# Attention with the top 32 keys and a highway layer: score tiles that are kept, and a dependency of last-row products on one of two top-eight passes taken off

## The chip, the cores and the metric

The kernel runs on one core of one Trainium2 chip. The metric is the time of one execution on the device in microseconds; the time of a kernel is the median of several executions. Times inside an execution come from one profiled execution of it.

## The reference

Queries, keys and values have 8 batches of 8 heads of 576 rows of 64 numbers. For each query row only the 32 largest scores take part in the softmax. The result of all heads, 4608 rows of 512, goes through a highway layer with two 512x512 weights.

```python
scores = scale * np.matmul(q, k.transpose(0, 1, 3, 2))
kth = np.partition(scores, -top_k, axis=-1)[..., -top_k:-top_k + 1]
mask = scores >= kth
scores = np.where(mask, scores, -1000000000.0)
scores = scores - np.max(scores, axis=-1, keepdims=True)
attn = np.exp(scores)
attn = attn / (np.sum(attn, axis=-1, keepdims=True) + 1e-09)
x = np.matmul(attn, v)          # then heads side by side: [4608, 512]
H = np.maximum(x @ w_h, 0.0)
T = 1.0 / (1.0 + np.exp(-(x @ w_t + b_t)))
out = T * H + (1.0 - T) * x
```

## The kernel before

**Units and pairs.** 576 query rows are four blocks of 128 rows and a last block of 64. A unit is what fills 128 partitions: a full block of one head, or the last 64 rows of two heads, one on partitions 0 to 63 and one on 64 to 127. Two units make a pair, and the text calls them the first and the second item of the pair. A batch has 16 pairs of full blocks and then 2 pairs of last rows, 18 in all; the kernel has 144 pairs, of which 16 are pairs of last rows.

**The score tile.** A pair's scores are written by TensorE into one PSUM tile `xs` of three banks of 512 numbers. The first item has columns 0 to 575: all of the first bank, and 64 columns of the middle one. The second item has the last 576 columns: 64 of the middle bank, and all of the third. There are two such tiles, taken in turn from the pool `xps`, so pair g has the tile that pair g - 2 had.

**One step.** The kernel is a pipeline with one step per pair, written out by hand; the program keeps the order in which it is written (`tc.manual_schedule`). In step i each engine does, in this order among others:

- TensorE (PE): the mask matmuls of pair i (`mask_add`, L419), which add a mark to all scores above a threshold; the products of probabilities and values of pair i - 3 (L509); matmuls without a use that keep its clock up (`spare`, L279); transposes of keys or queries for the next batch (L251); the score products of pair i + 2 (`scores`); one piece of the highway layer (L537); spares again.
- VectorE (DVE): twelve top-eight instructions over 96 columns each for pair i + 1 (`segs`, L358); a full top-eight over all 576 columns of each item of pair i (`below`, L432, two MAX8 in a row, first item first); the threshold of pair i + 1 (`refine`, L375 to L391); the selection of the 32nd score (L438, L451); the masked probabilities of pair i - 1 (L471).
- ScalarE (ACT): the exponentials of pair i (L424), the copy of the scores of pair i + 1 from PSUM (L353), the marks of pair i + 1 (`mask_count`, L406), the comparison for pair i - 1 (L454), copies of PE's other results (L523 for the value products, L252 for transposes, L624 and L648 for the highway layer).
- GpSimd (POOL): comparisons, the element-wise part of the highway layer, and the issue of some DMAs. SyncE issues most DMAs, the transposing ones for probabilities and for the layer's input `xT` among them.

**Around the change.** `below` of pair i needs the mask matmuls of pair i. It is the last reader of pair i's score tile: its first MAX8 reads the first and the middle bank, its second the middle and the third. Directly behind it in program order `start_scores(i + 2)` calls `scores`, which takes the tile anew for pair i + 2. A tile taken from a pool waits until all that used its predecessor is done; so the first product waits for both MAX8 of `below` and for PE's own mask matmuls.

For a pair of full blocks `scores` writes the two items in turn, 256 columns at a time (L311), and then the 64 end columns of both with one matmul (L322). For a pair of last rows it writes the first item, four matmuls of 256 columns into the first bank (L328; the profile counts each twice) and two of 64 columns into the middle bank (L339), and then the same for the second item into the third and the middle bank. The list `rest` and `declare_no_dep` in `segments` already let the twelve top-eight instructions of the first item start before the rest of the products is written; the tracker of dependencies otherwise goes by more than the columns that are used.

The lines of `finish` take the two score tiles again for the last highway blocks (`x1`, `x2`), and those of `begin` for the first transposes (`xa`). The code behind `tc.If` computes everything once more in a slower way where a check at the end asks for it, and is not run with these inputs.

Of the kernel before, what the change touches and what calls it, by code (L numbers as in the profile page):

```python
# [11 lines left out]
FP32 = mybir.dt.float32  # L12
# [14 lines left out]
def kernel(  # L27
# [10 lines left out]
    nc = tc.nc  # L38
    P = nc.NUM_PARTITIONS
# [13 lines left out]
    BANK = 512  # L53
# [13 lines left out]
    pairs = [(u, u + 1) for u in range(0, NU, 2)]  # L67
# [10 lines left out]
    xpool = ctx.enter_context(tc.tile_pool(name="x", bufs=3))  # L78
    fpool = ctx.enter_context(tc.tile_pool(name="f", bufs=2))
    hpool = ctx.enter_context(tc.tile_pool(name="h", bufs=3))  # L80
    xps = ctx.enter_context(tc.tile_pool(name="xps", bufs=2, space=bass.MemoryType.PSUM))
    ops = ctx.enter_context(tc.tile_pool(name="ops", bufs=1, space=bass.MemoryType.PSUM))
    fps = ctx.enter_context(tc.tile_pool(name="fps", bufs=1, space=bass.MemoryType.PSUM))


    ident_f = consts.tile([P, P], FP32)
# [12 lines left out]
    TOP, THR, KTH = 0, 1, NPK + 1  # L99
    wall = consts.tile([P, NU + 2, NPK + 2], FP32)  # L100
# [174 lines left out]
    def spare(n):  # L275
        if "t" not in po:
            po.update(t=pso_tile(), n=0)
        for _ in range(n):
            nc.tensor.matmul(  # L279
                po["t"][:, 4 * DE : BANK],  # L280
                ident_b[:],
                cst[:, 0 : BANK - 4 * DE],
                start=True,
                stop=True,
                skip_group_check=True,
            )

    def prep_alloc(kd):
        kT = kqpool.tile([P, NP, MAIN], FP32, name="kT")
        qT = kqpool.tile([P, NP, S], FP32, name="qT")  # L290
        return kT, qT, kd
# [2 lines left out]

    def scores(pair, prep):
        kT, qT, kd = prep
        ps = xps.tile([P, 3 * BANK], FP32, tag="x", name="xs")
        heads2 = [units[u][2] for u in pair]  # L300
        qt = units[pair[0]][1]
        qs = qt * P
        MB = 2 * BANK
        rest = []
        RA, RB = BANK, 2 * BANK - rem
        if qt < nfull:
            hp = heads2[0][0] // 2
            for n0 in range(0, MAIN, 256):
                for s, mo in ((0, 0), (1, MB)):
                    r = s * D  # L310
                    mm = nc.tensor.matmul(  # L311
                        ps[:, mo + n0 : mo + n0 + 256],
                        qT[r : r + D, hp, qs : qs + P],
                        kT[r : r + D, hp, n0 : n0 + 256],
                        start=(n0 == 0),
                        stop=True,
                        skip_group_check=True,
                    )
                    if s:
                        rest.append(mm)  # L320
            ends = ps[:, BANK:MB].rearrange("p (a n) -> p a n", n=rem)[:, 0 :: BANK // rem - 1, :]
            rest.append(nc.tensor.matmul(ends, qT[:, hp, qs : qs + P], kd[:, hp, :], start=True, stop=True))  # L322
        else:
            for (mo, ro), hh in zip(((0, RA), (MB, RB)), heads2):
                hp = hh[0] // 2
                for n0 in range(0, MAIN, 256):
                    for r in (0, D):
                        mm = nc.tensor.matmul(  # L328
                            ps[r : r + rem, mo + n0 : mo + n0 + 256],
                            qT[r : r + D, hp, qs : qs + rem],  # L330
                            kT[r : r + D, hp, n0 : n0 + 256],
                            start=(n0 == 0),
                            stop=True,
                            skip_group_check=True,
                        )
                        if mo:
                            rest.append(mm)
                for r in (0, D):
                    mm = nc.tensor.matmul(  # L339
                        ps[r : r + rem, ro : ro + rem],  # L340
                        qT[r : r + D, hp, qs : qs + rem],
                        kd[r : r + D, hp, r : r + rem],
                        start=(mo == 0),
                        stop=True,
                        skip_group_check=True,
                    )
                    rest.append(mm)
        both = bass.AP(tensor=ps.tensor, offset=ps[:].offset, ap=[ps[:].ap[0], [3 * BANK - S, 2], [1, S]])
        return ps[:, 0:S], ps[:, 3 * BANK - S : 3 * BANK], both, rest
# [49 lines left out]
    def biases(g):  # L399
        return nc.gpsimd.tensor_tensor(be[:, g], wall[:, 2 * g : 2 * g + 2, TOP : KTH + 1 : KTH - TOP], fac[:], ALU.mult)  # L400
# [22 lines left out]
    def expo(u, sc, e):  # L423
        nc.scalar.activation(e, sc, AF.Exp, bias=tb(u), scale=scale)  # L424
        return e
# [3 lines left out]
        return [t[:, s, :] for s in range(2)] + [t]  # L429

    def below(u, ps):
        nc.vector.max(wall[:, u, THR + 1 : KTH], ps)  # L432


    def hits(pair):
# [83 lines left out]
    def pso_tile():  # L519
        return ops.tile([P, BANK], FP32, tag="po", name="pso")  # L520
# [192 lines left out]
    preps = {0: prep_alloc(kds[0])}  # L713
# [4 lines left out]
    st = {}  # L718
# [4 lines left out]
    def ensure_prep(b, hp):  # L723
        for it in ((b, hp, 0), (b, hp, 1), (b, 0, 7), (b, 0, 8)):
            if it not in done:
                done.add(it)
                prep_piece(stages[b], preps[b], *it[1:])()
# [10 lines left out]
    def start_scores(g):  # L738
        b = units[pairs[g][0]][0]
        for u in pairs[g]:  # L740
            for h in units[u][2]:
                ensure_prep(b, h // 2)
        st[g] = dict(ps=scores(pairs[g], preps[b]), sc=[None, None], et=[None, None], e=[None, None])
        st[g]["seg"] = 0
        st[g]["cand"] = cands[g % len(cands)]

    def copy_both(g):
        st[g]["sc"] = copy_scores(st[g]["ps"][2])


    def segs(g, n):
        if g >= NG:
            return
        for c in range(st[g]["seg"], min(2 * NSEG, st[g]["seg"] + n)):
            s, k = divmod(c, NSEG)
            segments(st[g]["cand"][:, s], st[g]["ps"][s], k, k + 1, () if s else st[g]["ps"][3])
        st[g]["seg"] += n
# [27 lines left out]
    def masks_of(g):  # L785
        pr = pairs[g]
        views = (st[g]["ps"][0], st[g]["sc"][1])
        st[g]["m"] = [mask_count(u, views[s]) for s, u in enumerate(pr)]

    def step(i):  # L790
# [5 lines left out]
        b, k_in = divmod(i, SPB)  # L796
# [15 lines left out]
        if live:  # L812
            pr = pairs[i]
# [18 lines left out]
        segs(i + 1, 2 * NSEG)  # L832
        if live:
            below(pr[0], st[i]["ps"][0])
            below(pr[1], st[i]["ps"][1])
        if live:
            st[i]["e"] = pair_tile("e")
            expo(pr[0], st[i]["sc"][0], st[i]["e"][0])
# [71 lines left out]
    def begin():  # L910
        done.update((0, hp, part) for hp in range(NP) for part in range(2))
        done.update(((0, 0, 7), (0, 0, 8)))
        piece = partial(prep_piece, stages[0], preps[0])
        dve = nc.vector.tensor_copy
        spare(21)
        xa = xps.tile([P, 3 * BANK], FP32, tag="x", name="xs")
        ev0 = piece(0, 3)
        ev1 = piece(0, 5, xa, dve)
        ev2 = piece(0, 4, po["t"], dve)
        ev1()  # L920
        ev0()
        ev2()
        piece(0, 2, xa[:, BANK : 2 * BANK], dve)()
        po.clear()
        start_scores(0)
        piece(0, 6, pso_tile())()
        evs = [piece(1, 0), piece(1, 5, pso_tile())]
        for ev in evs:
            ev()
        segs(0, 2 * NSEG)  # L930
        copy_both(0)
        start_scores(1)
        for _ in refine(0, st[0]["cand"]):
            pass
        biases(0)
        evs = [piece(2, 0), piece(2, 5, pso_tile())]
        masks_of(0)
        for ev in evs:
            ev()
        rest = [(0, 3, 0), (0, 3, 1), (0, 1, 6), (0, 2, 6)]  # L940
        done.difference_update(rest)
        to_prep.extend(rest)
        vs = loads_v(0, vbs[0])
        todo_v.extend(vs[H:] + vs[0:H] + loads_w() + [load_bt])
# [20 lines left out]
    def finish():  # L965
        i = NG - 1
        pr, pu = pairs[i], pairs[i - 1]
# [15 lines left out]
        def bank(tile, k):  # L983
            return tile[:, k * BANK : (k + 1) * BANK]
# [22 lines left out]
        cur["e"] = pair_tile("e")  # L1007
        for s, u in enumerate(pr):
            expo(u, cur["sc"][s], cur["e"][s])
        x1 = xps.tile([P, 3 * BANK], FP32, tag="x", name="xs")  # L1010
        project(bank(x1, 1), z["qt"], z["xT"], wt, True)
        blk_gate(z, bank(x1, 1))
        n = values_of(i - 2, 2 * DE)
# [4 lines left out]
        old["et"] = transposes(pu[0])  # L1018
        nc.vector.tensor_tensor(hit[:], hit[:], wall[:, pr[0] : pr[1] + 1, THR:KTH], ALU.mult)
        pick_b(pr, hit)  # L1020
        x2 = xps.tile([P, 3 * BANK], FP32, tag="x", name="xs")
        cur["et"] = halves(et_tile())
        turned = None
        for s, home in enumerate((bank(x2, 1), bank(x1, 0))):
# [47 lines left out]
    with tc.If(fine < 1):  # L1072
        with tc.For_i(0, B, 1) as bi:
# [21 lines left out]
            prep = prep_alloc(kds[0])  # L1095
# [4 lines left out]
            for pr in pairs[0 : NG // B]:  # L1100
                scs = copy_scores(scores(pr, prep)[2])
                for s, u in enumerate(pr):
                    b, qt, heads = units[u]
                    if heads[0] == 0:
                        xs = xpool.tile([P, H * DE], FP32, name="xs")
                    sc = scs[s]
# [10 lines left out]
                    e = pair_tile("e")[s]  # L1117
# [45 lines left out]
```

## Time and profile before

| | |
|---|---|
| median of 3 executions | 797.43 us (797.13 to 797.91) |
| the profiled execution | 797.43 us, of which the span of instructions is 795.7 us |
| busy DVE / ACT / PE / POOL | 767.3 / 756.3 / 693.0 / 564.8 us |
| busiest groups | L358 on DVE 298.0 us, L279 on PE 247.1 us, L457 on POOL 232.5 us, L424 on ACT 227.8 us, L432 on DVE 205.2 us |
| score products of last-row pairs | L328 33.0 us, L339 9.4 us of PE |
| mean granted clock of PE | 0.996 |

PE is TensorE's matmuls, PEld its weight loads, which overlap with matmuls; DVE is VectorE, ACT ScalarE, POOL GpSimd, SP SyncE. A row of a group has the line, the engine, the operation, what is written and read (output <- input), the count, then the busy time in us and the mean of one instruction in ns, then the idle time of the engine just ahead of these instructions and what ended most of it. A row of the list of waits has the one that waited, the one that it waited for, the us in total, how many times, and the longest. A row of the timeline has the start and the duration in us; several instructions in a row of the same kind are one entry ("x8"), and the brackets give the idle time ahead of it and what ended it. Where an instruction waits for several things, the row names the one that came last.

### The profile page before, as it was taken

The page shows a single profiled execution, that of the slowest core. Times are in us where ns is not written, and L with a number is a line of the kernel's source. Part 1 is how long each engine was busy: PE and PEld are TensorE (multiplying, and loading weights), DVE is VectorE, ACT ScalarE, POOL GpSimd, SP SyncE. Part 2 cuts the span into 40 slices and gives each one's busy share as a digit, 9 for nine tenths or more (in the row PEclk, how much of TensorE's full clock was granted, in tenths as well). Part 3 has the DMA queues.
Part 4 walks back from the last instruction along what each step waited for, and adds up shares of the span by engine and source line. Part 5 has one row for each costly group of instructions (what it writes and reads, how often), then busy time and mean ns, then how long its engine had stood idle before and what let it go on. Part 6 is the DMA issues. An engine that isn't in the chain of part 4 may idle for free.

```text
span 795.7 us, 20350 instructions
## 1 busy us (share of the span) xinstructions
PE 693.0 (87%) x6459; PEld 494.6 (62%) x6459; DVE 767.3 (96%) x3947; ACT 756.3 (95%) x1401; POOL 564.8 (71%) x750
## 2 busy tenths in 40 slices
PE   8889988888988888888997889888998888988884
PEld 6666766566656666566665666656666666666552
DVE  6999999999999999999999999999999999999996
ACT  5999999999999999999999999999999999999984
POOL 2666867877778767787777876788777787776760
PEclk9999999999999999999999999999999999999998
DMA  6699967976899567987689866898677975565643
GB/s 125 88 136 172 127 125 140 159 127 87 140 157 156 104 99 135 159 136 117 106 146 159 133 110 111 154 154 127 107 129 146 162 118 96 97 113 98 114 85 89
DMA packets 341780, 100.32 MB, mean 126 GB/s; under 512 B 326048, under 2 KB 333856, under 8 KB 341664
## 3 DMA queue, kind: packets, MB, share of 16 engines
q1 hardware_dynamic: 286448, 79.14, 52.6%
q0 software_dynamic: 53536, 19.34, 22.5%
q8 instruction: 53, 0.87, 0.4%
q10 hardware_dynamic: 1680, 0.46, 0.3%
q14 instruction: 63, 0.52, 0.2%
HBM read 31.72 MB, written 9.44 MB: 52 GB/s over the span
## 4 chain that ended last, share of the span: by engine, by line
DVE 46%; ACT 32%; PE 16%; issue 2%; DMA 2%; SPq 0%; POOL 0%; DVEq 0%; ACTq 0%; POOLq 0%
DVE cand L358 16%; DVE wall L432 15%; ACT m L406 9%; ACT e L424 8%; ACT sc L353 6%; DVE ep L471 6%; ACT r L454 4%; PE xs L328 4%; PE fp L537 3%; PE pso L279 3%; PE xs L419 2%; PE xs L311 2%; DMA xT<-xb 2%; ACT xs L523 2%; DVE en L382 1%
## 5 line engine op out<-in xcount | busy, mean ns | idle before, releaser
L358 DVE MAX8 cand<-xs 128x8 f32<-128x96 f32 x1728 | 298.0, 252 | 0.4 <-PE xs L311 0.2
L279 PE MATMUL pso<-cst,ident_b 128*128 128x252 bf16 x1841 | 247.1, 272 | 41.8 <-ACT xs L523 39.7
L457 POOL TENSOR_SCALAR r<-sc,wall 128x576 bf16<-128x576 f32 x135 | 232.5, 1722 | 0.0
L424 ACT ACTIVATE e<-sc,be 128x576 bf16<-128x576 f32 x288 | 227.8, 791 | 0.1
L279 PEld LDWEIGHTS <-ident_b 128*128 128x128 bf16 x1841 | 173.5, 98 | 80.7 <-issue 48.9
L432 DVE MAX8 wall<-xs 128x8 f32<-128x576 f32 x288 | 205.2, 756 | 13.3 <-PE xs L419 12.1
L311 PE MATMUL xs<-kT,qT 64*128 64x256 f32 x1024 | 145.3, 400 | 34.0 <-DVE high L375 26.0
L353 ACT COPY sc<-xs 128x1152 f32<-128x1152 f32 x144 | 161.7, 1123 | 0.2
L311 PEld LDWEIGHTS xs<-kT,qT 64*128 64x128 f32 x1024 | 93.0, 186 | 65.5 <-issue 39.3
L406 ACT ACTIVATE m<-xs,wall 128x576 int8<-128x576 f32 x144 | 108.1, 751 | 9.8 <-DVE wall L391 8.6
L471 DVE TENSOR_TENSOR ep<-e,r 128x1024 bf16<-128x1024 bf16 (+2 forms) x236 | 116.4, 493 | 0.3 <-issue 0.2
L448 POOL TENSOR_TENSOR hit<-hit,wall 128x18 f32<-128x18 f32 x143 | 32.1, 225 | 113.5 <-DVE hit L438 113.5
L419 PE MATMUL xs<-m,ident_b 128*128 128x512 bf16 (+1 forms) x576 | 104.7, 285 | 9.0 <-ACT m L406 6.8
L406 ACT ACTIVATE m<-sc,wall 128x576 int8<-128x576 f32 x144 | 112.5, 781 | 0.0
L454 ACT ACTIVATE r<-sc,be 128x576 bf16<-128x576 f32 x143 | 111.0, 776 | 0.0
L509 PEld LDWEIGHTS <-et 128*128 128x128 bf16 (+1 forms) x1600 | 68.6, 100 | 19.9 <-issue 3.5
L400 POOL TENSOR_TENSOR be<-wall,fac 128x4 f32<-128x4 f32 x144 | 29.0, 201 | 71.9 <-DVE ep L471 52.0
L509 PE MATMUL pso<-vb,et 128*128 128x65 bf16 (+1 forms) x1600 | 74.4, 194 | 1.0 <-DMA et<-ep 1.0
L419 PEld LDWEIGHTS <-ident_b 128*128 128x128 bf16 x576 | 51.1, 98 | 35.5 <-issue 13.9
L322 PEld LDWEIGHTS xs<-kd,qT 128*128 128x128 f32 x256 | 38.1, 188 | 42.5 <-issue 42.1
L322 PE MATMUL xs<-kd,qT 128*128 128x128 f32 x256 | 62.5, 326 | 0.0
L625 POOL TENSOR_TENSOR s<-h,x 128x512 f32<-128x512 f32 (+1 forms) x37 | 42.8, 1157 | 1.0 <-ACT h L624 1.0
(128 smaller groups left out, 1005.8 us busy)
## 6 DMA issues: line engine op xcount, KB each, us to landing
kin<-in_k_dram SPq DMA_DIRECT2D x64, 128.0 KB, 3.2
qin<-in_q_dram SPq DMA_DIRECT2D x62, 128.0 KB, 3.1
out_dram<-s SPq DMA_DIRECT2D x30, 256.0 KB, 3.1
s<-h POOLq DMA_DIRECT2D x29, 256.0 KB, 3.8
xb<-x POOLq DMA_DIRECT2D x30, 128.0 KB, 2.7
vb<-in_v_dram POOLq DMA_DIRECT2D x28, 128.0 KB, 3.9
et<-ep SPq DMA_TRANSPOSE x143, 3.9
vb<-in_v_dram POOLq DMA_DIRECT2D x24, 64.0 KB, 3.0
```

The lines of the kernel that those rows point to most:

```text
L279: nc.tensor.matmul(po["t"][:, 4 * DE : BANK], ident_b[:], cst[:, 0 : BANK - 4 * DE], start=True, stop=True, skip_group_check=True,)
L311: mm = nc.tensor.matmul(ps[:, mo + n0 : mo + n0 + 256], qT[r : r + D, hp, qs : qs + P], kT[r : r + D, hp, n0 : n0 + 256], start=(n0 == 0), ...
L353: nc.scalar.copy(sc[:], both)
L358: ins = nc.vector.max(cand[:, s, :], sc[:, s * SEG : (s + 1) * SEG])
L406: nc.scalar.activation(m1[:].bitcast(I8)[:, 1 : 2 * S : 2], ps, AF.Sign, bias=wall[:, u, THR : THR + 1], scale=ABOVE, accum_out=csum[:, u ...
L419: nc.tensor.matmul(ps[:, s0:s1], ident_b[:], m1[:, s0:s1], start=False, stop=True, skip_group_check=True)
L424: nc.scalar.activation(e, sc, AF.Exp, bias=tb(u), scale=scale)
L432: nc.vector.max(wall[:, u, THR + 1 : KTH], ps)
L454: nc.scalar.activation(r, sc, AF.Relu, bias=eb(u), scale=BIGK)
L457: nc.gpsimd.tensor_scalar(r, sc, kth(u), None, ALU.is_ge)
L471: return nc.vector.tensor_tensor(out[:, :, c0:c1], e[:, :, c0:c1], r[:, :, c0:c1], ALU.min)
L509: nc.tensor.matmul(pso[r0 : r0 + ql, col : col + DE], ets[s][:, c, gi * P2 : gi * P2 + ql], vb[:, h, vc, :], start=(c == 0), stop=(c == nc ...
```

## The change

The two score tiles are made once and kept; pair g takes tile g mod 2 (`pair[0] // 2 % 2`). So a write to a tile no longer waits for the release of the tile before it, but for those earlier instructions that the tracker of dependencies finds for that write. In pairs of last rows, the four matmuls that write the first item's bank (the `mo == 0` case of L328) are then declared independent of one instruction: the second MAX8 of `below` of the pair two before, which `below` now returns for that. They still wait for its first MAX8. The end columns (L339), which lie in the middle bank, and all that follows are not declared so. In pairs of full blocks nothing is declared.

```diff
-    xps = ctx.enter_context(tc.tile_pool(name="xps", bufs=2, space=bass.MemoryType.PSUM))
+    xps = ctx.enter_context(tc.tile_pool(name="xps", bufs=1, space=bass.MemoryType.PSUM))
...
+    xss = [xps.tile([P, 3 * BANK], FP32, name=f"xs{i}") for i in range(2)]
...
-    def scores(pair, prep):
+    def scores(pair, prep, other=None):
+        def ahead(mm):
+            if other is not None:
+                tc.declare_no_dep(mm.ins, other.ins, reason="another bank")
+
         kT, qT, kd = prep
-        ps = xps.tile([P, 3 * BANK], FP32, tag="x", name="xs")
+        ps = xss[pair[0] // 2 % 2]
...
                         if mo:
                             rest.append(mm)
+                        else:
+                            ahead(mm)
...
     def below(u, ps):
-        nc.vector.max(wall[:, u, THR + 1 : KTH], ps)
+        return nc.vector.max(wall[:, u, THR + 1 : KTH], ps)
...
-        st[g] = dict(ps=scores(pairs[g], preps[b]), sc=[None, None], et=[None, None], e=[None, None])
+        st[g] = dict(ps=scores(pairs[g], preps[b], st[g - 2]["below"] if g > 1 else None), sc=[None, None], et=[None, None], e=[None, None])
...
             below(pr[0], st[i]["ps"][0])
-            below(pr[1], st[i]["ps"][1])
+            st[i]["below"] = below(pr[1], st[i]["ps"][1])
...
-        xa = xps.tile([P, 3 * BANK], FP32, tag="x", name="xs")
+        xa = xss[1]
...
-        x1 = xps.tile([P, 3 * BANK], FP32, tag="x", name="xs")
+        x1 = xss[i % 2 ^ 1]
...
-        x2 = xps.tile([P, 3 * BANK], FP32, tag="x", name="xs")
+        x2 = xss[i % 2]
```

## The prediction

> **What bounds the kernel now.** I read the page first, for who is busy, then its chain of work that ended last, then the group of the full top-eight.
>
> ```profile
> span 795.7 us, 20350 instructions
> PE 693.0 (87%) x6459; PEld 494.6 (62%) x6459; DVE 767.3 (96%) x3947; ACT 756.3 (95%) x1401; POOL 564.8 (71%) x750
> DVE 46%; ACT 32%; PE 16%; issue 2%; DMA 2%; SPq 0%; POOL 0%; DVEq 0%; ACTq 0%; POOLq 0%
> L432 DVE MAX8 wall<-xs 128x8 f32<-128x576 f32 x288 | 205.2, 756 | 13.3 <-PE xs L419 12.1 <-PE pso L509 0.7 <-ACT kT L252 0.2
> ```
>
> DVE is the bound of most of the span: it is idle for 795.7 - 767.3 = 28.4 us only. Of these, 13.3 us lie in one place, ahead of `below` (L432), and 12.1 us of them end with the mask matmuls of `mask_add` (L419). So there are stretches where PE is late and DVE stands. The list of waits says who is late there, and the windows of two steps show the change of the bound.
>
> ```profile
> DVE wall L432 <- PE xs L419: 12.1, 25, 1.1
> PEld xs L328 <- DVE wall L432: 4.6, 8, 0.9
> PEld xs L328 <- PE fp L251: 2.3, 7, 0.6
> PEld xs L328 <- issue: 1.1, 1, 1.1
> ```
>
> ```profile
> 471.50:483.10 11.60, 10.54 (x107) 7.25 (x107) 10.53 (x55) 11.18 (x21) 8.44 (x13) 1.00 0.80 129
> 483.10:493.47 10.37, 9.33 (x87) 6.32 (x84) 10.37 (x54) 10.12 (x19) 6.77 (x10) 1.00 0.53 95
> ```
>
> (Columns: length, then PE, PEld, DVE, ACT, POOL busy.) The first window holds the two steps of the fifth batch in which products of last-row pairs are issued, the second the two steps behind. Behind, DVE is busy for all of 10.37 us. In the first the steps take 11.60 us with DVE busy for 10.53: 1.07 us are lost, in each batch about as much. The timeline of that window shows how:
>
> ```profile
> 471.50 1.41 DVE L432 MAX8 wall<-xs 128x8 f32<-128x576 f32 x2
> 472.09 0.20 PEld L279 LDWEIGHTS <-ident_b 128*128 128x128 bf16 x2 [0.79 <-issue]
> 472.96 0.62 PEld L328 LDWEIGHTS xs<-kT,qT 64*64 64x64 f32 x8 [0.67 <-DVE wall L432]
> 473.67 0.35 PEld L339 LDWEIGHTS xs<-kd,qT 64*64 64x64 f32 x4
> ...
> 474.99 0.79 ACT L406 ACTIVATE m<-sc,wall 128x576 int8<-128x576 f32 x1
> 475.73 0.53 PEld L279 LDWEIGHTS <-ident_b 128*128 128x128 bf16 x4
> 476.27 0.45 PEld L419 LDWEIGHTS <-ident_b 128*128 128x128 bf16 x4
> 476.38 0.65 PE L419 MATMUL xs<-m,ident_b 128*128 128x512 bf16 x4
> 477.14 1.43 DVE L432 MAX8 wall<-xs 128x8 f32<-128x576 f32 x2 [0.35 <-PE xs L419]
> 477.94 0.47 PEld L251 LDWEIGHTS fp<-ident_f,qin 128*128 128x128 f32 x4
> 478.69 0.65 PEld L328 LDWEIGHTS xs<-kT,qT 64*64 64x64 f32 x8 [0.28 <-PE fp L251]
> ...
> 483.10 1.43 DVE L432 MAX8 wall<-xs 128x8 f32<-128x576 f32 x2 [0.72 <-PE xs L419]
> 483.35 0.38 ACT L523 COPY xs<-pso 128x260 f32<-128x260 f32 x1 [0.64 <-PE pso L509]
> ```
>
> PE stands for 0.67 us until the second Max of `below` ends at 471.50 + 1.41 = 472.91. From 472.96 on its weight loads show no other idle time up to 478.69; what it lost is still missing when DVE wants the masked scores at 477.14 (0.35 idle) and again at 483.10 (0.72). Only the waits ahead of L328 are to be had; the rest of PE's work there is work.
>
> **The change, part by part.** Both programs issue the same instructions in the same order on every engine; only waits and completion signals differ. No DMA and no queue moves.
>
> *The first item's products (L328, first four of a pair, 16 pairs).* They now wait for the first Max of `below` two pairs back, not for both. The first ends 0.756 us after the start (row of L432): 471.50 + 0.76 = 472.26, with the same 0.05 us of hand-over as now (472.91 to 472.96) 472.31. But PE must be free. How soon a product's load follows when it has nothing to wait for stands in two rows of other steps:
>
> ```profile
> 101.58 0.47 PEld L251 LDWEIGHTS fp<-ident_f,qin 128*128 128x128 f32 x4
> 102.21 0.73 PEld L311 LDWEIGHTS xs<-kT,qT 64*128 64x128 f32 x8 [0.17 <-DVE neg L379]
> ```
>
> ```profile
> 483.77 0.74 PEld L279 LDWEIGHTS <-ident_b 128*128 128x128 bf16 x7 [0.56 <-issue]
> 484.72 0.73 PEld L311 LDWEIGHTS xs<-kT,qT 64*128 64x128 f32 x8 [0.21 <-DVE high L375]
> ```
>
> Behind transposes (L251) 102.21 - 102.05 = 0.16 us, behind spares (L279) 0.21 us; `below` had long ended in both. This is the floor. Fifth batch: 0.67 - 0.21 = 0.46 and 0.28 - 0.16 = 0.12, together 0.58 us. DVE can follow: the first step gives it at most 0.35, but PE keeps the rest, and at 483.10 there are 0.35 + 0.72 to take. ACT can follow too: its mask's main instruction ends at 474.99 + 0.79 = 475.78, ahead of the mask matmuls at 476.38 - 0.46 = 475.92, and at 483.35 it has 0.64 idle. First batch:
>
> ```profile
> 90.02 0.62 PEld L328 LDWEIGHTS xs<-kT,qT 64*64 64x64 f32 x8 [0.30 <-DVE wall L432]
> 95.74 0.66 PEld L328 LDWEIGHTS xs<-kT,qT 64*64 64x64 f32 x8 [0.29 <-PE fp L251]
> ```
>
> Both stand behind transposes: 0.59 - 0.32 = 0.27. Last batch:
>
> ```profile
> 758.02 1.42 DVE L432 MAX8 wall<-xs 128x8 f32<-128x576 f32 x2
> 759.50 0.62 PEld L328 LDWEIGHTS xs<-kT,qT 64*64 64x64 f32 x8 [0.91 <-DVE wall L432]
> 762.91 0.65 PE L419 MATMUL xs<-m,ident_b 128*128 128x512 bf16 x4
> 764.02 1.43 DVE L432 MAX8 wall<-xs 128x8 f32<-128x576 f32 x2 [0.70 <-PE pso L509]
> 765.57 0.66 PEld L328 LDWEIGHTS xs<-kT,qT 64*64 64x64 f32 x8 [1.11 <-issue]
> 769.99 1.43 DVE L432 MAX8 wall<-xs 128x8 f32<-128x576 f32 x2 [0.73 <-PE xs L419]
> ```
>
> Here the first Max limits: 758.02 + 0.76 + 0.05 = 758.83, gain 0.67. The next `below` comes 764.02 - 763.56 = 0.46 us behind the mask matmuls, where the fifth batch took 477.14 - 477.03 = 0.11; I let these 0.35 us stay, so it gains 0.35. Then the products go at 764.02 - 0.35 + 0.81 = 764.48, 1.09 early, and DVE has 0.35 + 0.73 = 1.08 to take: 1.1 us (0 of the 0.35 staying: 1.4).
>
> The other five batches: all idle time ahead of L328 is 4.6 + 2.3 + 1.1 = 8.0; less the first, fifth and last batch (0.59, 0.95, 2.02) 4.44 in ten waits, less five times 0.16 + 0.21: 2.6 us. Sum: 0.27 + 0.58 + 1.1 + 2.6 = 4.55, taken as 4.5. Behind each pair of steps DVE is busy throughout, so the lead stays.
>
> *The end blocks (L339).* They write the middle bank, which the second Max reads, and get a wait of their own, 16 in all. Queued behind it on PE are the second item's products, one FFN piece, spares and the mask matmuls that the next `below` awaits. The load of L339 comes 473.67 - 472.96 = 0.71 us behind L328's; moved by 0.46 it is at 473.21, behind the Max's end at 472.91. Only in the last batch do both ends meet (to 0.05 us). A wait already met costs between nothing and an event instruction's length:
>
> ```profile
> L328 PEldq EVENT_SEMAPHORE  x8: 51/51/51, 95.7 to 765.5; - x8
> L311 PEldq EVENT_SEMAPHORE  x65: 51/51/51, 16.4 to 754.3; - x65
> L432 DVE MAX8 wall<-xs x288: 745/756/769, 14.9 to 775.7; 128x8 f32<-128x576 f32 x144
> ```
>
> At most 16 x 0.05 = 0.8 us; I take 0, by the nearest row: L419, whose matmuls wait for ACT's masks, begins its loads 0.01 us behind the spares (475.73 + 0.53 = 476.26). [...]
>
> *Signals of the Max pairs.* In these 16 steps each Max is now signalled by itself; before, one signal came behind the second. Two Max of 0.756 take 1.42 us, so they overlap by 0.09. Lost everywhere, that is 16 x 0.09 = 1.4 us; the other end is 0, which I take: the instructions do not change.
>
> *Kept tiles.* PE's waits for its own earlier matmuls fall away: the event instructions above, 8 ahead of L328 (inside the floor) and all but one of 65 ahead of L311. The latter are worth nothing where DVE is busy throughout. They count at most in those of the 25 waits of `below` outside these batches: fewer than twelve, 0.6 us. Four new waits on PE and one each on DVE and ACT, at the edges: 0.05 each at most, 0.3; taken as 0.
>
> The profiled execution took 797.43 us, which is the median: 797.43 - 4.5 = 792.9.
>
> **The rivals.**
>
> *The lead is given back.* Three times the FFN piece waits for a transposed input, and that transfer is then on the chain:
>
> ```profile
> PE fp L537 <- DMA xT<-xb: 2.6, 3, 1.1
> 715.43 3.83 DMA xT<-xb
> ```
>
> If the transfers land at fixed times, each stall swallows the lead won so far. The last is at 715, so only the last batch's 1.1 remains: 796.3. Against it: the transfer is issued behind work that moves forward as well.
>
> *Nothing happens.* If the first Max's signal in effect comes with the second's, products start as now: 797.4. For it: the two Max overlap. Against it: their starts lie some 0.67 us apart (1.42 - 0.756), far more than the 0.12 to 0.46 that are asked for outside the last batch.
>
> *Slower.* The second Max now reads banks 1 and 2 of a tile whose bank 0 PE is writing. If that stretches it, DVE, the bound, pays: twice as long is 16 x 0.756 = 12.1 us, 797.4 - 4.5 + 12.1 = 805.0. It decides from 4.5 / 16 = 0.28 us per Max. Against it: all 288 Max lie within 745 and 769 ns, with PE writing other banks beside many of them, as the transposes at 477.94 do. No row shows PE writing the same tile. [...]
>
> **How the numbers follow.** Forecast 0.70; given back 0.12; nothing 0.10; slower 0.08. The range: its low end has 4.5, the last batch's 0.35, the 0.6 of the event instructions and about half a stall of L537 less (2.6 / 3 = 0.87 each): 797.4 - 5.9 = 791.5. Its high end: both bounds lost (1.4 + 0.8) leave 2.3, 795.1, and with 0.3 for the new waits and some lead given back 795.8. A measurement tells about 0.2% (1.6 us) from no change, so faster means below 795.8. Giving back is faster only in part, say 0.08 of its 0.12: faster 0.78, same 0.04 + 0.10 = 0.14, slower 0.08.
>
> **What would show it.** Right: the idle time ahead of L328 falls from 8.0 to about 3.2 us; L328's first load stands before the end of the Max pair in the later batches, L339's behind it; `below` waits for L419 for about 8 us, not 12.1; L432 stays at 756 ns; the two steps of the fifth batch last 11.0 us. Wrong: a new idle time ahead of L339; longer Max; longer waits for xT; or a start of L328 as now.

## The result and the profile after

The changed kernel takes 794.38 us (median of 7 executions, 792.91 to 795.89), the kernel before 797.84 us beside it (7 executions, 797.13 to 798.37). The ratio is 0.9957, with an interval of 0.9945 to 0.9969: about 3.4 us faster (2.5 to 4.4 by the interval), where 4.5 were forecast. The profiled execution took 794.38 us, the median.

In the changed kernel the lines have moved: L311 is now L316, L322 is L327, L328 is L333, L339 is L346, L358 is L365, L419 is L426, L432 is L439, L537 is L544, L251 is L252, L279 is L280. First the page: span, busy time, and the shares of the chain of work that ended last; then the group of the full top-eight.

```profile
span 792.7 us, 20191 instructions
PE 686.7 (87%) x6369; PEld 488.1 (62%) x6459; DVE 766.0 (97%) x3947; ACT 755.2 (95%) x1401; POOL 564.8 (71%) x750
...
ACT 39%; DVE 36%; PE 17%; DMA 4%; issue 2%; SPq 1%; POOL 0%; DVEq 0%; another core or an unknown queue 0%; ACTq 0%; POOLq 0%
...
L439 DVE MAX8 wall<-xs 128x8 f32<-128x576 f32 x288 | 204.1, 749 | 11.3 <-PE xs L426 5.1
```

The span is 3.0 us shorter. PE's busy time can't be compared: 90 of its 6459 matmuls left no record in this trace. DVE does the same work; a MAX8 takes 749 ns instead of 756, so it is not stretched. The share of the DMAs on the chain has doubled, from 2% to 4%: the first sign of what went otherwise than forecast. The list of waits of the changed kernel tells both halves:

```profile
...
PEld L544 <- DMA xT<-xb: 6.8, 7, 1.5
PE fp L544 <- DMA xT<-xb: 6.7, 7, 1.5
...
DVE wall L439 <- PE xs L426: 5.1, 12, 1.1
...
DVE wall L439 <- ACT tt L655: 2.6, 5, 0.6
...
PEld xs L333 <- DVE wall L439: 1.7, 9, 0.2
PEld xs L333 <- issue: 1.3, 7, 0.2
```

The idle time ahead of the first products of last-row pairs (L333) is 1.7 + 1.3 = 3.0 us, where it was 8.0 and 3.2 were forecast.

`below` is idle for 11.3 us in all, where it was 13.3. The rows that name L426 and ACT add up to 7.7 us (in four of the five waits put down to ACT the mask matmuls end 0.11 us ahead, as the next view shows for one), but other rows name other lines of PE; in e11_after_again, a second profile of the same kernel, the waits that follow the end of the mask matmuls so closely add up to 9.8 us. So `below` waits for PE for some 10 us instead of 12.1, where about 8 were forecast. The highway piece waits seven times for its transposed input, 6.7 us, where it waited three times, 2.6 us; 0.77, 1.10 and 0.39 us of the waits of `below` stand right behind late inputs that are new.

The longest row of the whole list that is new, 48.1 us of L316 waiting for `below`, is no new idle time: there were 65.5 us ahead of L311, most of it put down to `issue`, and there are 65.1 ahead of L316.

The timeline of the fifth batch:

```profile
468.65 1.41 DVE L439 MAX8 wall<-xs 128x8 f32<-128x576 f32 x2
469.24 0.20 PEld L280 LDWEIGHTS <-ident_b 128*128 128x128 bf16 x2 [0.79 <-issue]
469.65 0.62 PEld L333 LDWEIGHTS xs<-kT,qT 64*64 64x64 f32 x8 [0.21 <-DVE wall L439]
470.35 0.35 PEld L346 LDWEIGHTS xs<-kd,qT 64*64 64x64 f32 x4
...
471.87 2.07 DVE L365 MAX8 cand<-xs 128x8 f32<-128x96 f32 x12
473.06 0.65 PE L426 MATMUL xs<-m,ident_b 128*128 128x512 bf16 x4
473.86 1.41 DVE L439 MAX8 wall<-xs 128x8 f32<-128x576 f32 x2
474.62 0.47 PEld L252 LDWEIGHTS fp<-ident_f,qin 128*128 128x128 f32 x4
475.25 0.63 PEld L333 LDWEIGHTS xs<-kT,qT 64*64 64x64 f32 x8 [0.17 <-issue]
475.96 0.35 PEld L346 LDWEIGHTS xs<-kd,qT 64*64 64x64 f32 x4
478.88 0.65 PE L426 MATMUL xs<-m,ident_b 128*128 128x512 bf16 x4
479.64 1.43 DVE L439 MAX8 wall<-xs 128x8 f32<-128x576 f32 x2 [0.57 <-ACT tt L655]
```

L333 starts at 469.65, 0.41 us before the Max pair ends at 468.65 + 1.41 = 470.06, and 0.21 us behind the spares; the second time it starts 0.17 us behind the transposes. That is the floor, in both places. L346 comes at 470.35, behind the pair's end and 0.70 us behind L333, as L339 came 0.71 us behind L328 (472.96 to 473.67). The two steps take 479.64 - 468.65 = 10.99 us; 11.0 were forecast. The last row names ACT, but the mask matmuls end at 478.88 + 0.65 = 479.53, 0.11 us before `below` starts, as in the kernel before: it is PE that comes last.

In the last batch one of the late inputs falls into the pair of steps itself:

```profile
755.85 1.41 DVE L439 MAX8 wall<-xs 128x8 f32<-128x576 f32 x2
756.65 0.62 PEld L333 LDWEIGHTS xs<-kT,qT 64*64 64x64 f32 x8 [0.24 <-DVE wall L439]
...
759.51 0.55 PEld L544 LDWEIGHTS <-xT 128*128 128x128 bf16 x4 [0.82 <-DMA xT<-xb]
...
760.82 0.65 PE L426 MATMUL xs<-m,ident_b 128*128 128x512 bf16 x4
761.58 1.43 DVE L439 MAX8 wall<-xs 128x8 f32<-128x576 f32 x2 [0.44 <-PE xs L426]
```

The products start 0.80 us behind `below`, where they started 1.48 behind it before (758.02 to 759.50). The highway piece between them and the mask matmuls then waits 0.82 us for its input, and the 0.68 us are gone.

### The profile page after: what moved, and what is told of

The parts are those of the page before. It is cut to its first block, busy times and chain, and to the rows that moved or that the text cites. A ratio compares the mean times of both kernels' runs of the same rounds, so it can differ in the third digit from the quotient of the medians.

```text
span 792.7 us, 20191 instructions
## 1 busy us (share of the span) xinstructions
PE 686.7 (87%) x6369; PEld 488.1 (62%) x6459; DVE 766.0 (97%) x3947; ACT 755.2 (95%) x1401; POOL 564.8 (71%) x750
## 4 chain that ended last, share of the span: by engine, by line
ACT 39%; DVE 36%; PE 17%; DMA 4%; issue 2%; SPq 1%; POOL 0%; DVEq 0%; another core or an unknown queue 0%; ACTq 0%; POOLq 0%
ACT m L413 12%; DVE cand L365 12%; DVE wall L439 11%; ACT e L431 9%; ACT sc L360 7%; ACT r L461 5%; DVE ep L478 5%; PE pso L280 4%; PE xs L333 4%; DMA xT<-xb 3%; PE fp L544 3%; PE xs L426 2%; ACT xs L530 2%; PE pso L516 1%; DVE en L389 1%
## 5 line engine op out<-in xcount | busy, mean ns | idle before, releaser
L365 DVE MAX8 cand<-xs 128x8 f32<-128x96 f32 x1728 | 297.4, 246 | 0.4 <-PE xs L316 0.2
L280 PE MATMUL pso<-cst,ident_b 128*128 128x252 bf16 x1841 | 247.1, 272 | 42.0 <-ACT xs L530 39.6
L280 PEld LDWEIGHTS <-ident_b 128*128 128x128 bf16 x1841 | 173.5, 98 | 80.6 <-issue 48.7
L439 DVE MAX8 wall<-xs 128x8 f32<-128x576 f32 x288 | 204.1, 749 | 11.3 <-PE xs L426 5.1
L316 PE MATMUL xs<-kT,qT 64*128 64x256 f32 x1024 | 145.3, 402 | 28.9 <-DVE wall L439 26.2
L316 PEld LDWEIGHTS xs<-kT,qT 64*128 64x128 f32 x1024 | 88.3, 186 | 65.1 <-DVE wall L439 48.1
L413 ACT ACTIVATE m<-xs,wall 128x576 int8<-128x576 f32 x144 | 108.3, 752 | 11.2 <-DVE wall L398 9.8
L426 PE MATMUL xs<-m,ident_b 128*128 128x512 bf16 (+1 forms) x512 | 92.0, 274 | 11.7 <-ACT m L413 10.5
L426 PEld LDWEIGHTS <-ident_b 128*128 128x128 bf16 x576 | 51.4, 97 | 39.2 <-issue 17.3
L327 PEld LDWEIGHTS xs<-kd,qT 128*128 128x128 f32 x256 | 38.1, 188 | 42.5 <-issue 42.1
L327 PE MATMUL xs<-kd,qT 128*128 128x128 f32 x256 | 62.5, 326 | 0.0
```

What stands on the lines that cost most here:

```text
L280: nc.tensor.matmul(po["t"][:, 4 * DE : BANK], ident_b[:], cst[:, 0 : BANK - 4 * DE], start=True, stop=True, skip_group_check=True,)
L316: mm = nc.tensor.matmul(ps[:, mo + n0 : mo + n0 + 256], qT[r : r + D, hp, qs : qs + P], kT[r : r + D, hp, n0 : n0 + 256], start=(n0 == 0), ...
L365: ins = nc.vector.max(cand[:, s, :], sc[:, s * SEG : (s + 1) * SEG])
L413: nc.scalar.activation(m1[:].bitcast(I8)[:, 1 : 2 * S : 2], ps, AF.Sign, bias=wall[:, u, THR : THR + 1], scale=ABOVE, accum_out=csum[:, u ...
L426: nc.tensor.matmul(ps[:, s0:s1], ident_b[:], m1[:, s0:s1], start=False, stop=True, skip_group_check=True)
L439: return nc.vector.max(wall[:, u, THR + 1 : KTH], ps)
```

## The experiments

All labels below are kernels of their own, each timed in rounds beside the kernel before on the same chip. Two quantities recur. **Pair steps** are the two steps of a batch in which last-row products are issued, from a `below` to the second `below` after it, summed over the eight batches in a profiled execution; **other** is the rest of the time from the first `below` to the end of the last pair steps. Late inputs are the steps in which the highway piece (L537 before, L544 after, one line further where the use is later) waited for xT; two numbers stand where its weight loads and its matmuls differ.

| kernel | median us | ratio to before, interval | pair steps | other | late inputs |
|---|---|---|---|---|---|
| before | 797.84 | | 93.25 | 661.79 | 3 |
| after | 794.38 | 0.9957 (0.9945 to 0.9969) | 88.91 | 663.19 | 7 |
| e12_before_again | 797.43 | 0.9999 (0.9990 to 1.0008) | 93.24 | 661.74 | 3 to 4 |
| e11_after_again | 794.86 | 0.9962 (0.9949 to 0.9975) | 88.90 | 663.43 | 6 to 7 |
| e1_kept_only | 797.55 | 0.9995 (0.9986 to 1.0004) | 92.20 | 663.23 | 6 to 7 |
| e10_first_only | 795.59 | 0.9973 (0.9963 to 0.9984) | 90.12 | 664.08 | 7 |
| e2_before_later | 795.59 | 0.9973 (0.9961 to 0.9984) | 91.15 | 662.41 | 0 |
| e3_after_later | 791.32 | 0.9918 (0.9904 to 0.9931) | 87.50 | 661.20 | 0 |
| e5_before_late2 | 796.19 | 0.9985 (0.9976 to 0.9994) | 91.22 | 661.72 | 0 |
| e6_kept_late2 | 794.52 | 0.9966 (0.9952 to 0.9979) | 90.42 | 661.34 | 0 |
| e7_after_late2 | 791.06 | 0.9921 (0.9908 to 0.9935) | 87.49 | 661.21 | 0 to 1 |
| e8_after_lean_late2 | 790.20 | 0.9909 (0.9894 to 0.9924) | 86.69 | 661.34 | 1 |
| e9_before_lean | 790.56 | 0.9916 (0.9902 to 0.9929) | 86.87 | 661.46 | 3 |
| e4_after_lean | 789.22 | 0.9892 (0.9876 to 0.9907) | 84.35 | 662.32 | 2 |

My theory was that the change gains in the pair steps what was forecast, and that late transfers of xT take a part back. The rivals: the gain in the pair steps is smaller, because `below` is held by something else; or the kept tiles cost time by themselves.

### Which part of the change does what

**e1_kept_only** keeps the tiles, but declares nothing:

```diff
-        st[g] = dict(ps=scores(pairs[g], preps[b], st[g - 2]["below"] if g > 1 else None), ...
+        st[g] = dict(ps=scores(pairs[g], preps[b]), ...
```

> The two score tiles are kept as in the changed kernel, but no product is declared independent of the second MAX8. Theory (the early products make the gain, kept tiles only take 51 ns event instructions away where PE is the bound): the idle time ahead of L328 stays near 7.5 us, and the time falls by 0.5 to 1.3 us, to about 797 us. Rival (keeping the tiles is what makes the gain): the time falls by about 3.5 us, to 794.4 us.

No measurable difference from before, where 0.5 to 1.3 us were expected. Its list of waits:

```profile
DVE wall L439 <- PE xs L426: 10.0, 21, 1.1
...
PEld xs L333 <- DVE wall L439: 7.2, 16, 0.9
...
PE fp L544 <- DMA xT<-xb: 5.6, 7, 1.5
```

L333 waits for `below` in all 16 pairs, 7.2 us against the 8.0 of before, so the early start needs the declaration. But two things happen that cancel: the pair steps become 93.25 - 92.20 = 1.05 us shorter, and the other steps 663.23 - 661.79 = 1.44 us longer, with the late inputs already at seven. Late inputs thus come with the kept tiles, before any product starts early.

**e10_first_only** declares the first of the two last-row pairs of a batch only:

```diff
-... st[g - 2]["below"] if g > 1 else None)
+... st[g - 2]["below"] if g % SPB == SPB - 2 else None)
```

> The changed kernel, but only the first of the two last-row pairs of a batch has its products declared independent. Theory (PE keeps what it wins in the first step and uses it in the second only if the second pair may start early too): the two steps of batches 5 to 7 last 11.1 to 11.25 us (11.61 before, 10.99 with both), their sum over 8 batches is 90 to 91 us (93.25 before, 92.20 with kept tiles alone, 88.91 with both), and the time is 795.5 to 796.5 us. Rival (the first step's lead is worth its full size without the second): 10.99 + 0.12 = 11.1 us or less in batches 5 to 7 and a sum under 90 us.

The pair steps sum to 90.12 us, as expected, but not in the pattern that I expected: in batches 5 to 7 they take 11.06 us, only 0.07 more than with both declared (10.99), while in the third and the last batch the second declaration is worth 0.4 to 0.5 us. So the first step by itself gives more than the 0.35 us that I had taken for its limit. The reason stands in the rows of the top-eights ahead of `below`. In the kernel before:

```profile
474.72 2.07 DVE L358 MAX8 cand<-xs 128x8 f32<-128x96 f32 x12
```

They end at 476.79, and `below` starts at 477.14, 0.35 us later. In the changed kernel they end at 471.87 + 2.07 = 473.94, and `below` has started at 473.86, 0.08 us before that. So the first of the two Max overlaps the top-eight before it by 0.08 us here, where DVE doesn't wait; in the kernel before, where it waits, the overlap is lost as well as the idle time that the profile shows: 0.35 + 0.08 = 0.43 us.

### Do late transfers take back a part?

**e2_before_later** and **e3_after_later** are the two kernels with the use of each xT put one step later; everything else stays. They leave out one piece of work: the gate (one projection, its tanh and the store of 128 output rows) of the last block but one of the last batch.

```diff
+    turned = []
...
-            ready.extend([hh, tt])
+            turned.extend([hh, tt])
...
+        ready.extend(turned)
+        turned.clear()
```

> The kernel before, with the matmuls of the highway layer that need a transposed input (xT) put in line one step later, so that the transfer has about 5 us more to land. Both theories: the waits of L537 for xT (2.6 us in 3 in the profile before) go, and with them up to 2.3 us of the waits of below for PE; the time is 795.5 to 797.5 us.

> The changed kernel with the same later use of xT. Theory (the lead of 4.3 us won in the 16 steps is partly given back at late xT transfers, 7 waits in place of 3): with those waits gone, the distance to the kernel before with the later use is 4.3 to 5.2 us. Rival (the lead is given back for another reason, or is not won): the distance stays at 3.5 us or less.

e3 is 795.59 - 791.32 = 4.27 us faster than e2, where after and before lay 3.4 apart. From the list of waits of e3:

```profile
PEld xs L333 <- DVE wall L439: 2.5, 9, 0.4
...
DVE wall L439 <- PE xs L426: 1.6, 7, 0.3
...
PEld xs L333 <- issue: 1.4, 7, 0.2
```

No row of the highway piece (L545 there) waits for a transfer any more. Moving the use also moves the highway pieces into other steps, so that the pair steps of e2 are not those of before. **e5**, **e6** and **e7** therefore repeat this with all work done (later use in the first seven batches only), for before, kept tiles only, and after:

```diff
-            ready.extend([hh, tt])
+            (turned if b < B - 1 else ready).extend([hh, tt])
```

> As the second experiment (the kernel before, with xT used one step later), but only in the first seven batches, so that all pieces of the highway layer are issued; the second and third experiment leave out the gate of the last but one block of the last batch. Both theories: 795.6 us, give or take 0.6, few waits for xT.

> Kept tiles alone (no product declared independent), with the same later use of xT. In the first experiment kept tiles alone moved nothing, with 7 waits for xT of 5.6 us in its profile against 3 of 2.6 us in that of before. Theory: there they won 0.5 to 1.0 us (an event instruction less in the step behind each pair of last-row steps and ahead of L328) and late transfers took it; here, without late transfers, the time is 0.5 to 1.0 us under the kernel before with the later use. Rival: kept tiles are worth nothing, the distance is within 0.3 us.

> The changed kernel with the same later use of xT. Theory: 4.3 us (3.8 to 5.0) under the kernel before with the later use, of which the early products make 3.3 to 4.0. Rival (the 4.3 us between the second and third experiment were made by the missing piece): under 3.5 us.

Now the kept tiles gain 796.19 - 794.52 = 1.67 us by themselves, and all of the change 796.19 - 791.06 = 5.13, both more than expected; the profiled spans, one execution each, lie 793.8 - 792.8 = 1.0 and 793.8 - 789.9 = 3.9 us apart. With late inputs out of the way the change is worth 3.9 to 5.1 us, with them 3.0 (spans) to 3.4, as the theory says. It is not a clean test: with the later use the pair steps hold other highway pieces and give 91.22 - 87.49 = 3.73 us instead of 4.34, and the other steps become 0.51 shorter instead of 1.40 longer.

The steps of before and after, one by one, say it more directly. Outside the pair steps four steps have a late input that they didn't have before; they grow by 0.36, 0.84, 1.17 and 0.78 us. One step has lost its late input and shrinks by 1.18 us. Together that is 1.97 us longer, and all other steps together are 0.57 us shorter. A fifth new late input is the one of the last batch's pair steps.

**e11_after_again** and **e12_before_again** are the two kernels unchanged, to see whether the late inputs are chance.

> The changed kernel once more, for a second profile of it. If the late xT transfers belong to this program, there are again 6 or 7 waits of L544 for xT of about 6.5 us, in the same steps; if they belong to the single execution, their number and places differ.

> The kernel before once more, for a second profile. If late xT transfers belong to the program, there are again 3 waits of about 2.6 us in the same steps (two of them in steps 55 and 132); if to the single execution, number and places differ.

From the lists of waits, e11 and then e12:

```profile
PEld L544 <- DMA xT<-xb: 6.4, 7, 1.5
PE fp L544 <- DMA xT<-xb: 5.0, 6, 1.3
```

```profile
PEld L537 <- DMA xT<-xb: 3.4, 4, 1.3
PE fp L537 <- DMA xT<-xb: 2.5, 3, 1.1
```

They belong to the program: the late steps are the same ones as in the first profiles, but for one wait of 0.3 us that is new in e12. One of the late inputs that only the changed kernel has, in its timeline, and then the same step in the kernel before:

```profile
522.64 1.20 SPq L609 DMA_TRANSPOSE xT<-xb  x1
527.12 0.55 PEld L544 LDWEIGHTS <-xT 128*128 128x128 bf16 x4 [1.49 <-DMA xT<-xb]
```

```profile
524.96 1.23 SPq L602 DMA_TRANSPOSE xT<-xb  x1
528.17 0.55 PEld L537 LDWEIGHTS <-xT 128*128 128x128 bf16 x4
```

The use stands 527.12 - 522.64 = 4.48 us behind the issue in the one and 528.17 - 524.96 = 3.21 in the other: the transfer itself took longer, while the use would have come at 4.48 - 1.49 = 2.99. The times from DMA to landing of all these transposes (min, median, max), after and then before:

```profile
DMA to landing us min/median/max: 2.4/3.0/5.1
```

```profile
DMA to landing us min/median/max: 2.3/2.9/4.7
```

The medians are alike, but single transfers are not. In order of time, the five new late inputs landed 2.9, 4.3, 4.4, 3.8 and 4.1 us after the DMA in the changed kernel, and the same five 2.9, 2.5, 3.2, 3.0 and 2.6 us in the kernel before; the one that is no longer late landed after 3.1 us instead of 4.7. So four of the five transfers became 0.8 to 1.8 us slower. For three of them (the second to the fourth) that alone makes the wait, as the use came 3.2 to 3.3 us behind the issue before. At the fifth, in the last batch, the use also comes sooner, 3.3 us behind the issue instead of 4.1; at the first, it comes sooner and the transfer is as before. Why other transfers are slow with kept tiles was not tried and stays open.

### What else holds PE back there

The mask matmuls (L426) that `below` awaits stand directly behind four spares, matmuls without a use, 0.53 us in the kernel before (the row at 475.73). **e4_after_lean** takes these four out where last-row products are issued:

```diff
-        spare(4 if late else 10)
+        last_rows = i + 2 < NG and units[pairs[i + 2][0]][1] == nfull
+        spare(0 if last_rows and late else 4 if late else 10)
```

> The changed kernel without the four spare matmuls behind the products of last-row pairs (16 steps, 64 matmuls of no use). Theory (PE is still the bound in the second of each two steps, DVE stands 0.57 us ahead of below there): the mask matmuls come up to 0.43 us sooner in that step, ACT allows about 0.35 of it, 8 times: the time falls by 2 to 3 us against the changed kernel, to about 792 us. Rival (ACT is the bound by now): it stays within 0.5 us of the changed kernel, 794.4 us. If the lower load on PE lowers its granted clock below 0.99, it may also lose.

789.22 us, 5.2 us below the changed kernel and the fastest of all; 2 to 3 were expected. The pair steps give 88.91 - 84.35 = 4.56 us, and the other steps, with two late inputs in place of seven, 663.19 - 662.32 = 0.87. **e9_before_lean** makes the same edit in the kernel before.

> The kernel before without the four spare matmuls behind the products of last-row pairs, nothing else. Theory (PE is late in these steps, whatever the cause): below comes 0.35 us sooner after the first and 0.78 us sooner after the second of the two steps, about 6 us over the 8 batches, of which ACT takes back some 1 us in the step behind, as it did in the changed kernel without these spares: 792 to 793.5 us; the distance that the change still makes (789.2 us with it) is 2.5 to 4 us. Rival (PE is not the bound in these steps): within 0.5 us of the kernel before.

790.56 us: this one line alone wins 6.95 us, twice what the change wins, with all the old waits in place. From its list of waits and its timeline:

```profile
DVE wall L432 <- PE xs L419: 5.0, 15, 0.8
...
PEld xs L328 <- DVE wall L432: 4.6, 8, 0.9
```

```profile
467.11 1.41 DVE L432 MAX8 wall<-xs 128x8 f32<-128x576 f32 x2
...
468.57 0.63 PEld L328 LDWEIGHTS xs<-kT,qT 64*64 64x64 f32 x8 [0.68 <-DVE wall L432]
...
471.34 0.56 PEld L419 LDWEIGHTS <-ident_b 128*128 128x128 bf16 x4
...
472.32 1.43 DVE L432 MAX8 wall<-xs 128x8 f32<-128x576 f32 x2
```

PE still stands 0.68 us ahead of L328, but the mask matmuls' loads follow 471.34 - 467.11 = 4.23 us behind `below` instead of 476.27 - 471.50 = 4.77, and DVE no longer waits in the first step. My expectation, 792 to 793.5, was too slow, and the distance between e4 and e9 was expected at 2.5 to 4 us; it is 790.56 - 789.22 = 1.3, from two chips, with intervals that overlap (up to 0.9907 and from 0.9902), so it may be less. Once the spares are out, little is left for the earlier start to win. The mean granted clock of PE is 0.996 in e4 and in e9, as with all spares. **e8_after_lean_late2** joins e4's edit and e7's.

> The same without the four spare matmuls behind the products of last-row pairs. The fourth experiment won 5.2 us against the changed kernel where 2 to 3 were expected. Theory (2 to 3 us of it were PE's time, the rest fewer late xT transfers: 2.6 us of waits in its profile against 6.7): here, with few late transfers in either, the distance to the changed kernel with the later use is 2.0 to 3.5 us, 788 to 789 us. Rival (all 5.2 us were PE's time): 786 us.

Only 791.06 - 790.20 = 0.9 us below e7, where 2.0 to 3.5 were expected. The two edits don't add. With the later use other highway pieces fall into the pair steps, and in the fourth to the seventh batch these last the same 10.9 to 11.2 us in e7 and e8; in the last batch one input is 1.7 us late. The fifth batch's two steps in e8:

```profile
466.81:472.55 5.74, 4.90 (x62) 3.35 (x59) 5.74 (x27) 5.53 (x13) 4.38 (x7) 1.00 0.64 80
472.55:477.69 5.14, 4.80 (x49) 2.92 (x47) 5.14 (x29) 4.80 (x9) 3.75 (x6) 1.00 0.66 118
```

(Columns: length, then PE, PEld, DVE, ACT, POOL busy.) DVE is busy for all of 5.74 and 5.14 us, as it already is in e7 with the spares. PE isn't late there any more, so there is nothing left for the spares to give.

## Why the prediction was right, and what was mis-sized

**The first item's products: right.** The idle time ahead of L328 was forecast to fall from 8.0 to 3.2 us and fell to 3.0. In the pair steps the sum is, batch by batch:

| | forecast us | measured us |
|---|---|---|
| first batch | 0.27 | 0.28 |
| fifth batch | 0.58 | 0.61 |
| last batch | 1.1 | 0.85 |
| the other five | 2.6 | 2.60 |
| sum | 4.5 | 93.25 - 88.91 = 4.34 |

e1 splits the sum: 1.05 us come with the kept tiles, the other 3.29 with the declaration. The forecast put all of it down to the products' start, with the eight event instructions ahead of L328 inside its floor. The kept tiles give about 0.10 us in the second step of each batch (in the fifth, the idle time ahead of the products goes from 0.28 to 0.22 us with them and to 0.17 with the declaration) and 0.28 us in the first step of the last batch.

That the sum is so near is in part luck, for in the last batch the gain comes by another way. The forecast let the 0.35 us by which `below` came later behind the mask matmuls stay (0.46 against 0.11), and took 0.35 from the earlier products. In fact `below` comes 761.58 - 761.47 = 0.11 us behind them, so the 0.35 didn't stay, and the products' lead of 0.68 went into the late input shown above. This first step is 5.72 us long with and without the declaration (6.00 before).

**"Behind each pair of steps DVE is busy throughout, so the lead stays": the step that failed.** The steps outside the pairs became 663.19 - 661.79 = 1.40 us longer (1.69 in e11 against e12), and the late inputs rose from three to seven, five new ones and one gone; without late inputs the other steps don't grow (661.72 in e5, 661.21 in e7). This is the "lead is given back" rival, given a chance of 0.12, but not as it priced it: it let three known stalls swallow the whole lead up to 715 us, where in fact two of these stalls stay as long as they were, one goes, and new ones appear, most of them because their transfers land later. I had read the three stalls of before as the whole risk. What I should have read is the slack of the inputs that did not stall: with uses some 3 us behind the issue and landings between 2.3 and 4.7 us, each of them could become late. 4.34 - 1.40 = 2.94 us is what the profiled spans show (795.7 - 792.7); the medians give 3.4.

**"Worth nothing where DVE is busy throughout" (the event instructions ahead of L311): a little too low.** They were taken as 0, with 0.6 us as a bound. With kept tiles the second step behind the pair steps becomes shorter (5.22 to 5.14 us in e1, in the median of the batches), and without late inputs the steps outside the pairs become 661.72 - 661.34 = 0.38 us shorter in all, from e5 to e6.

**"The rest of PE's work there is work": wrong.** Four spares stand directly ahead of the mask matmuls, 0.53 us in the row at 475.73 that the prediction shows. Leaving these 64 matmuls out gains 6.95 us (e9), where the waits ahead of L328 give 4.34 in the pair steps.

**"The first step gives it at most 0.35": too low** by the lost overlap of 0.08: in batches 5 to 7 it gives 5.64 - 5.20 = 0.44 us, in e10 as in the changed kernel.

**The new waits of L339: right at 0.** L346, which now waits for `below` in each of the 16 pairs, begins as soon behind L333 as L339 did behind L328 (0.70 and 0.71 us). These rows show no delay, and the time missing from the forecast lies at xT.

**The signals of the Max pairs: right at 0.** Two MAX8 still take 1.41 us together.

**The slower rival** needed 0.28 us more per Max. From the summary of this line's instructions (min, median, max in ns):

```profile
L439 DVE MAX8 wall<-xs x288: 737/746/768, 14.9 to 772.6; 128x8 f32<-128x576 f32 x144
```

The longest is no longer than before (769). In the changed kernel PE writes the first bank beside the second Max for 0.07 us or more in ten of the 16 steps, for up to 0.61 us, and there this Max takes 743 to 749 ns (747 to 757 before, in all 16). **The "nothing happens" rival** fell with L333's start ahead of the pair's end, in these ten steps.

## What to carry to other kernels

When the bounding engine waits for a late one, look first at what the late engine does without need just ahead of what is awaited: here 64 useless matmuls cost twice what a finer dependency gained. A lead won in one place can be lost at transfers behind it, so compare each transfer's issue-to-use distance with the whole range of landing times (here some 3 us with 2.3 to 5.1), also where nothing stalls yet. And read the cost of a stall as its idle time plus the overlap that it breaks (here 0.35 + 0.08 us).

## What was not expected of the hardware

**A wait cost more than its idle time on DVE.** In the kernel before and in the changed one, two MAX8 of 0.756 and 0.746 us (the medians) take 1.41 to 1.43 us, and a DVE instruction that waits for nothing starts some 0.08 us before the recorded end of the one ahead. A wait that was met late lost that overlap (`below` at 477.14, 0.35 us behind the end at 476.79); one that was met in time kept it (`below` at 473.86, 0.08 us ahead of the end at 473.94).

**PE's clock did not need those spares.** With 64 of the 1841 left out the mean granted clock stayed at 0.996 (e4, e9). It did fall where PE had no more work: in the kernel before the last matmul ends at 786.97 us, and the granted clock is 1.00 up to 789 and 0.50 from 790 to 795; in the changed kernel the last matmul ends at 783.95, and the clock is 1.00 up to 785 and 0.50 from 786 to 794. No run leaves the other 1777 spares out.

**Two engines on two banks of one tile** did not disturb each other: from 469.65 on PE writes the first bank while the second Max reads the other two until 470.06, and the Max pair takes 1.41 us as before (471.50).
